# Attention and a gated feed-forward on one core: where batch 1's queries and two of its x are turned, and when the later batches are loaded

## The chip, the cores and the metric

The kernel runs on one core of a Trainium2 chip. The metric is the time of one execution on the device in microseconds (us), lower is better. TensorE multiplies matrices, VectorE, ScalarE and GpSimd work on tiles, SyncE issues transfers. The profile calls them PE (and PEld for its weight loads), DVE, ACT, POOL and SP.

## What is computed

q, k and v have the shape 4 x 8 x 768 x 64 (batch, head, position, width). Each position sees its neighbours less than 16 positions away, and 24 block summaries: the elementwise maximum of 32 keys, with the mean of 32 values. The result goes through two weight matrices with a gate between them.

```
k_sum = k.reshape(B, H, nb, block, D).max(axis=3)
v_sum = v.reshape(B, H, nb, block, D).mean(axis=3)
scores_l = scale * q @ k.T                 # kept where |i - j| < 16
scores_s = scale * q @ k_sum.T + log(32)
a = softmax(concat(scores_l, scores_s))
x = a @ concat(v, v_sum)                   # to (B * S, H * D) = (3072, 512)
h = x @ w_in                               # 512 -> 2048
out = (h / (1 + exp(-beta * h))) @ w_out   # 2048 -> 512
```

## The kernel before

The order on every engine is written by hand. Heads are taken in pairs, so each batch has four pairs g = 0..3, and a pair's two heads of width 64 fill the 128 partitions. Batch 0 has a path of its own at the start (lines 622 to 690). The loop over b at line 723 then runs the feed-forward of batch b as a main list of TensorE pieces, and between these pieces, at times given as numbers, it puts the attention of batch b + 1 (at_time, line 726). A piece with a smaller number is written earlier; the numbers only order the program, and each engine takes its instructions in that order and waits for their operands. Two kinds of main pieces alternate: the rising ones (h_group, h_ps at line 545, followed by the gate on ScalarE at line 557) and the falling ones (o_part, o_ps at line 576, followed by a copy and an output store at lines 595 and 596). For batch 0 the lists start at dn0 (the falling matmuls of the first half), up1 and dn1 (rising and falling of the second half); for the later batches the rising stage starts at 0 and the falling one at up.

The attention of a pair takes these steps:

- Loads. k, q and v come through POOL's queue, which also converts them to bf16. load_run (line 91) brings long runs: a partition holds six consecutive positions, both heads in one transfer. load_row (line 97) brings one position of one head per row, in two transfers per pair. load_v (line 103) brings v shifted by 16 rows, ve. load_1 (line 692) issues batch 1's loads, load_next (line 714) those of batches 2 and 3.
- Keys and queries are turned so that the width stands on the partitions: kw and qt. In batch 1 this is done on TensorE (turn, line 265: 12 transposes into pk or pq, line 276), and a copy (line 277) carries them out. In batches 2 and 3, cross (line 286) does it with two DMA transposes on SP's queue, one for k, one for q.
- max_k and rows_k (lines 293 and 303) make the block maxima and place them beside the keys, on VectorE.
- copy_v (line 312) makes vo, a second copy of v shifted by 16 rows across partitions. In batch 1 by eight DMAs on SP's queue, in batches 2 and 3 by VectorE.
- mean_v (line 319) takes the block means on TensorE (vm_ps, line 324); rows_v (line 348) places them with eight copies on VectorE (line 353).
- scores (line 449) multiplies queries with keys (s_ps, line 459) and takes the exponential on ScalarE (line 460), mask (line 480) multiplies with the band on VectorE (line 482), av (line 494) multiplies with v (av_ps, line 502), norm (line 506) divides into x_nat (line 512).
- x_transpose (line 515) turns x for the feed-forward, xT. Batch 1: six transposes on TensorE per pair (px, line 526) and a copy on ScalarE. Batches 2 and 3: one DMA transpose on SP's queue (line 521).

All of batch 1's k and q share the buffers k_all and q_all with batch 2's, so batch 2's loads of a pair wait until batch 1's have been turned. POOL's loads take eight completion semaphores in turn, so each of them waits for the landing of the eighth before it.

Of the kernel before, what the change touches and what calls it, by code (L numbers as in the profile page):

```python
# [12 lines left out]
def kernel(  # L13
# [10 lines left out]
    nc = tc.nc  # L24
# [18 lines left out]
    npair = H // 2  # L43
# [42 lines left out]
    nat = {}  # L86
    dve, act, pool = nc.vector.tensor_copy, nc.scalar.copy, nc.gpsimd.tensor_copy
# [3 lines left out]
    def load_run(nm, b, g, n=1, p0=0, p1=P, key=None):  # L91
        t = qk_bufs[nm][p0:p1, 2 * g:2 * (g + n)]
        nc.gpsimd.dma_start(out=t, in_=(k_run if nm == "k" else q_run)[b, p0:p1, 2 * g:2 * (g + n)])  # L93
        for i in range(n):
            nat[(key or nm, b, g + i)] = t[:, 2 * i:2 * i + 2]

    def load_row(nm, b, g):
        t = qk_bufs[nm][:, 2 * g:2 * g + 2].rearrange("p h f -> p (h f)").rearrange("p (c h d) -> p c h d", h=2, d=D)
        for h in range(2):
            nc.gpsimd.dma_start(out=t[:, :, h], in_=(k_row if nm == "k" else q_row)[b, g, :, h])  # L100
        nat[(nm, b, g)] = t

    def load_v(b, g):
        lo, hi = PC * g + 1, min(PC * (g + 1) + 1, HC)
        src = v_rows[b, lo * P - W:hi * P - W].rearrange("(c p) d -> p c d", p=P)
        nc.gpsimd.dma_start(out=ve_bufs[b % 2][:, lo:hi, 0:D], in_=src)  # L106
# [142 lines left out]
    def flat_k(b, g):  # L249
        return kw_of(b, g)[:, 0].rearrange("p c f -> p (c f)")  # L250
# [33 lines left out]
        turn(nm, b, g, flat_q(g)[:, lo:hi], copy, tag)  # L284

    def cross(b, g):
        kt, qn = nat.pop(("k", b, g)), nat.pop(("q", b, g))
        nc.sync.dma_start_transpose(out=flat_k(b, g)[:, W:W + S].rearrange("p (c f) -> p c f", f=P),
                                    in_=kt.rearrange("p c h d -> p (c h d)"))
        nc.sync.dma_start_transpose(out=qt_bufs[g].rearrange("p m r f -> p m (r f)"),  # L290
                                    in_=qn.rearrange("p c h d -> p (c h d)"))

# [222 lines left out]
    def x_transpose(key, m0, n, tag, copy):  # L515
        b, g = key[:2]
        if b not in xT:
            xT[b] = xt_pool.tile([P, k1, S], bf16, name="xT", tag="xT")
        x = x_nat.pop(key)
        if b > 1:  # L520
            nc.sync.dma_start_transpose(out=xT[b][:, g, :].rearrange("p (c f) -> p c f", f=P),
                                        in_=x.rearrange("p c h d -> p (c h d)"))
            return
        px = psum([P, n * P], bf16, "px", tag)
        for c in range(n):
            nc.tensor.transpose(px[:, c * P:(c + 1) * P], x[:, c].rearrange("p h d -> p (h d)"), identity)  # L526
        copy(out=xT[b][:, g, m0 * P:(m0 + n) * P], in_=px[:])
# [94 lines left out]
    for nm, n, copy, src in (("k", P, dve, k_f32), ("q", HP, act, q_f32)):  # L622
        t = nat[(nm, 0, 0)] = qk_bufs[nm][0:n, 0:2]
# [67 lines left out]

    def load_1(g):
        load_run("k", 1, g)
        load_run("q", 1, g)
        if g == npair - 1:
            load_v_first(1)
            load_v_last(1)
            for i in range(npair):
                load_v(1, i)

    GT, OT = 1.3, 0.865

    def run(main, side):
        side.sort(key=lambda z: z[0])
# [16 lines left out]
    for b in range(B):  # L723
        side = []

        def at_time(t, f, *a):
            side.append((t, lambda: f(*a)))

        us = [u for u in range(len(units)) if units[u][0] == b]
        main, t = [], 0.0  # L730
        if b == 0:
            starts = []
            for u in us:
                starts.append(t)
                for i in range(2 if u == 0 else 0, NG[u]):
                    main.append((t, lambda u=u, i=i: h_group(u, i)))
                    t += GT
                starts.append(t)
                todo = [(ms, q) for q in range(4) for ms in range(HM)] if u == 0 else [(ms, q) for ms in range(HM) for q in range(4)]
                for ms, q in todo:  # L740
                    main.append((t, (lambda ms=ms, q=q: o_quarter(0, ms, q)) if u == 0 else (lambda u=u, ms=ms, q=q: o_part(u, ms, q, 4))))
                    t += OT
            up0, dn0, up1, dn1 = starts
            us_rest = []
        else:
            us_rest = us
        for u in us_rest:
            for i in range(NG[u]):
                first = range(k1 - 1, k1) if i < 2 else range(k1)
                main.append((t, lambda u=u, i=i, first=first: h_group(u, i, first)))  # L750
                t += GT
        up = t
        for u in us_rest:
            for ms in range(units[u][2] * HM):
                for p in range(4):
                    main.append((t, lambda u=u, ms=ms, p=p: o_part(u, ms, p, 4)))
                    t += OT
        if b + 1 < B:
            main += [(t + i, lambda i=i: h_group(us[-1] + 1, i, range(k1 - 1))) for i in range(2)]
        nxt = b + 1  # L760
        pairs = tuple(range(npair))
        if b == 0:
            def part(n, f, *a):
                at_time(dn0 + OT * (n - 0.5), f, *a)

            for g in pairs:
                at_time(0.1 + 1.3 * g, rows_k, 0, g, HM)
                at_time(dn0 - GT - 0.1 if g < 2 else dn0 - 0.4, prep_q, 0, g, dve, "q2")
                at_time(dn0 - 0.3, load_1, g)
                if g > 1:  # L770
                    at_time(dn0 - 2 * GT, copy_v, 0, g, HM, dve)
                    at_time(dn0 - 2 * GT, rows_v0, g, dve)
            part(-0.1, load_table, ACTF.Exp)
            for g in pairs:
                part((0.2, 3)[g // 2], scores2, g)
                part((1.1, 3.2)[g // 2], mask2, g)
            for n in range(k2):
                part((-0.05, 1, 3.1, 4.5)[n // 4], scale_w_out, n)
            for gg in range(2):
                key = (1, 2 * gg, 2)  # L780
                part((4, 6)[gg], av2, key)
                part((4, 6)[gg], norm_x, key, 1 + gg)
            part(7.5, turn_x, (1, 0, 2), act)
            part(9.5, turn_x, (1, 2, 2), act)
            part(9.6, load_table, ACTF.Silu)
            for g in pairs:
                t = up1 + 0.3 + 2.2 * g
                at_time(t, prep_k, 1, g)
                at_time(t, prep_q, 1, g)
                at_time(t + 0.5, max_k, 1, g)  # L790
                at_time(t + 0.5, rows_k, 1, g)
                at_time(up1 + 3.0, copy_v, 1, g, 0, nc.sync.dma_start)
                at_time(up1 + 8.7, rows_v, 1, g)
            at_time(up1 + 8.6, mean_v, 1, pairs)
            at_time(dn1 - 0.1, load_table, ACTF.Exp)

            s_at = [dn1 + OT * (n - 0.5) for n in (0, 3, 5, 6)]
            a_at = [dn1 + OT * (n - 0.5) for n in (5, 6, 8, 9)]
            x_at = [t + 2.5 * OT for t in a_at]
        elif nxt < B:  # L800
            for g in pairs:
                t = (0.65, 1.95, 5.85, 9.75)[g]
                at_time(t, copy_v, nxt, g)
                at_time(t, cross, nxt, g)
                at_time(3.9 + 3.9 * g, max_k, nxt, g)
                at_time(3.9 + 3.9 * g, rows_k, nxt, g)
            at_time(15.3, mean_v, nxt, pairs)
            for g in pairs:
                at_time(15.4, rows_v, nxt, g)
            s_at = [up + 4.0 * g for g in pairs]  # L810
            a_at = [up + 4.0 * (g + 1) for g in pairs]
        if nxt < B:
            for g in pairs:
                for par in range(2):
                    at_time(s_at[g], scores, nxt, g, par)
                    at_time(s_at[g], mask, nxt, g, par)
                at_time(a_at[g], av, (nxt, g), nch)
                at_time(a_at[g], norm, (nxt, g), nch)
                if nxt > 1:
                    at_time(a_at[g], x_transpose, (nxt, g), 0, nch, "big", dve)  # L820
                else:
                    at_time(x_at[g], x_transpose, (nxt, g), 0, nch, "t", act)
        if nxt + 1 < B:
            for g in pairs:
                at_time((up1 + 5.0 if b == 0 else 1.0) + (2.5 if b == 0 else 4.5) * g, load_next, nxt + 1, g)
        run(main, side)


# [28 lines left out]
```

## Time and profile before

| | |
|---|---|
| median of 3 runs | 216.81 us (216.42 to 216.91) |
| the profiled execution | 215.99 us, its span 214.3 us |
| busy, PE / ACT / DVE / POOL | 206.3 / 122.1 / 104.1 / 77.7 us |
| moved by DMA | 25.88 MB, mean 121 GB/s |
| rising matmuls (L545) | 85.6 us |
| falling matmuls (L576 and L607) | 73.1 + 11.5 us |

The span runs from the first to the last instruction. Rows of the chain give the start in us, the length and what ran or was waited for; rows of a timeline the same with engine, line, operation and operands. Transfers are shown by their issue, with the time to landing beside them.

### The profile page before, as it was taken

The page shows a single profiled execution, that of the slowest core. Times are in us where ns is not written, and L with a number is a line of the kernel's source. Part 1 is how long each engine was busy: PE and PEld are TensorE (multiplying, and loading weights), DVE is VectorE, ACT ScalarE, POOL GpSimd, SP SyncE. Part 2 cuts the span into 40 slices and gives each one's busy share as a digit, 9 for nine tenths or more (in the row PEclk, how much of TensorE's full clock was granted, in tenths as well). Part 3 has the DMA queues.
Part 4 walks back from the last instruction along what each step waited for, and adds up shares of the span by engine and source line. Part 5 has one row for each costly group of instructions (what it writes and reads, how often), then busy time and mean ns, then how long its engine had stood idle before and what let it go on. Part 6 is the DMA issues. An engine that isn't in the chain of part 4 may idle for free.

```text
span 214.3 us, 5128 instructions
## 1 busy us (share of the span) xinstructions
PE 206.3 (96%) x2115; PEld 115.9 (54%) x2134; DVE 104.1 (49%) x299; ACT 122.1 (57%) x170; POOL 77.7 (36%) x113
## 2 busy tenths in 40 slices
PE   7999989999999999999999999999999999999994
PEld 2567654556655556655545466555554466654442
DVE  5768939808899729475544426182454000002120
ACT  2775977197788587668443187757342477650000
POOL 7996989496799308976000000000000000000000
PEclk9999999999999999999999999999999999999999
DMA  6999999999999999999934358400433300001212
GB/s 155 175 144 195 198 206 207 201 176 239 186 157 170 141 123 147 148 137 138 167 98 137 86 127 135 85 3 0 135 89 86 110 29 0 3 0 49 99 49 98
DMA packets 84087, 25.88 MB, mean 121 GB/s; under 512 B 70224, under 2 KB 81120, under 8 KB 84064
## 3 DMA queue, kind: packets, MB, share of 16 engines
q0 software_dynamic: 60272, 13.34, 76.2%
q1 hardware_dynamic: 23504, 11.82, 24.7%
q10 hardware_dynamic: 288, 0.39, 0.6%
q8 instruction: 16, 0.26, 0.5%
q14 instruction: 7, 0.06, 0.1%
HBM read 27.27 MB, written 6.29 MB: 157 GB/s over the span
## 4 chain that ended last, share of the span: by engine, by line
PE 82%; DMA 9%; POOL 4%; issue 1%; DVE 1%
PE h_ps L545 34%; PE o_ps L576 34%; DMA w_out_sb<-in_moe_w_out_dram 6%; PE o_ps L607 5%; DMA w_in_sb<-in_moe_w_in_dram 3%; PE av_ps L502 3%; PE s_ps L459 3%; POOL ve L106 2%; PE pk L276 1%; PE px L526 1%; PE vm_ps L324 1%; PE pq L276 1%; POOL q_all L93 1%; PE av_ps L491 0%; POOL near L144 0%
## 5 line engine op out<-in xcount | busy, mean ns | idle before, releaser
L545 PE MATMUL h_ps<-xT,w_in_sb 128*128 128x384 bf16 x512 | 85.6, 326 | 0.0
L576 PE MATMUL o_ps<-w_out_sb,h_sb 128*128 128x512 bf16 (+2 forms) x336 | 73.1, 369 | 2.0 <-issue 1.7
L557 ACT ACTIVATE h_sb<-h_ps,beta_sb 128x768 bf16<-128x768 f32 (+1 forms) x80 | 59.2, 772 | 22.6 <-PE h_ps L545 22.4
L545 PEld LDWEIGHTS <-w_in_sb 128*128 128x128 bf16 x512 | 49.3, 98 | 33.0
L576 PEld LDWEIGHTS <-h_sb 128*128 128x128 bf16 x352 | 32.4, 98 | 35.2
L460 ACT ACTIVATE attn<-s_ps 128x768 bf16<-128x768 f32 x24 | 18.1, 808 | 10.4 <-PE s_ps L459 10.4
L595 DVE COPY o_sb<-o_ps 128x512 f32<-128x512 f32 x5 | 3.5, 691 | 38.5 <-PE o_ps L576 38.5
L595 ACT COPY o_sb<-o_ps 128x512 f32<-128x512 f32 x15 | 8.8, 587 | 18.5 <-PE o_ps L576 12.7
L106 POOL DMA_DIRECT2D ve<-in_v_dram x16 | 17.1, 1074 | 1.8 <-DMA k_all<-in_k_dram 0.9
L482 DVE TENSOR_TENSOR attn<-attn,band 128x768 bf16<-128x768 bf16 x24 | 13.1, 554 | 7.5 <-ACT attn L460 6.0
L100 POOL DMA_DIRECT2D k_all<-in_k_dram x16 | 13.7, 860 | 7.7 <-DMA kw<-k_all 5.8
L100 POOL DMA_DIRECT2D q_all<-in_q_dram x16 | 13.6, 857 | 4.4 <-DMA ve<-in_v_dram 3.3
L296 DVE TENSOR_TENSOR half<-kw 128x384 bf16<-128x384 bf16 x16 | 5.9, 367 | 15.2 <-DMA kw<-k_all 15.0
L607 PE MATMUL o_ps<-w_out_sb,h_sb 128*128 128x512 bf16 x45 | 11.5, 379 | 1.1 <-DVE w_out_sb L235 0.7
L511 DVE RECIPROCAL r<-av_ps 128x12 f32<-128x12 f32 x12 | 2.8, 232 | 19.6 <-PE av_ps L502 19.6
L277 DVE COPY qt<-pq 128x384 bf16<-128x384 bf16 (+1 forms) x11 | 7.5, 696 | 9.5 <-PE pq L276 8.7
L512 DVE TENSOR_TENSOR x_nat<-av_ps,r 128x768 bf16<-128x768 f32 x12 | 11.5, 957 | 0.4
L588 ACT COPY o_sb<-o_ps 128x384 f32<-128x384 f32 x1 | 0.5, 478 | 19.0 <-PE o_ps L576 19.0
L317 DVE COPY vo<-ve 64x780 bf16<-64x780 bf16 (+3 forms) x20 | 8.9, 445 | 0.4
L502 PEld LDWEIGHTS <-attn 128*64 128x64 bf16 x288 | 5.5, 111 | 5.1 <-issue 3.0
L306 DVE COPY kw<-kw 128x192 bf16<-128x192 bf16 (+2 forms) x32 | 7.5, 277 | 0.0
L607 PEld LDWEIGHTS <-h_sb 128*128 128x128 bf16 x48 | 4.3, 97 | 5.8 <-issue 0.9
(115 smaller groups left out, 200.3 us busy)
## 6 DMA issues: line engine op xcount, KB each, us to landing
out_dram<-o_sb SPq DMA_DIRECT2D x23, 256.0 KB, 2.2
ve<-in_v_dram POOLq DMA_DIRECT2D x12, 192.0 KB, 6.9
w_in_sb<-in_moe_w_in_dram POOLq DMA_DIRECT2D x8, 256.0 KB, 8.3
w_out_sb<-in_moe_w_out_dram POOLq DMA_DIRECT2D x4, 512.0 KB, 12.4
q_all<-in_q_dram POOLq DMA_DIRECT2D x17, 96.0 KB, 6.3
k_all<-in_k_dram POOLq DMA_DIRECT2D x16, 96.0 KB, 6.9
k_all<-in_k_dram POOLq DMA_DIRECT2D x5, 192.0 KB, 8.1
q_all<-in_q_dram POOLq DMA_DIRECT2D x5, 192.0 KB, 7.2
```

Of the source, the lines that this page charges most:

```text
L100: nc.gpsimd.dma_start(out=t[:, :, h], in_=(k_row if nm == "k" else q_row)[b, g, :, h])
L106: nc.gpsimd.dma_start(out=ve_bufs[b % 2][:, lo:hi, 0:D], in_=src)
L317: copy(out=dst, in_=src)
L460: nc.scalar.activation(out=a.rearrange("p m h f -> p h m f"), in_=sv, func=ACTF.Exp, scale=scale)
L482: nc.vector.tensor_mul(out=a, in0=a, in1=band[:, par])
L502: nc.tensor.matmul(ov[par * QT:(par + 1) * QT, h, m], a[:, par, m, h], t[:, PC * g + nch * h + m0 + m], start=True, stop=True)
L512: nc.vector.tensor_mul(out=x.rearrange("p m h d -> p h m d"), in0=ov[:, :, :, 0:D], in1=r[:, :, :, None].to_broadcast([P, 2, n, D]))
L545: nc.tensor.matmul(big[:, j, 0:MG], w_in_sb[:, ki, ni * P:(ni + 1) * P], xT[b][:, ki, tok:tok + MG], start=(ki == 0), stop=(ki == k1 - 1))
L557: nc.scalar.activation(out=hb.rearrange("p (k m) -> p k m", m=MG), in_=big[:, j:j + w, 0:MG], func=ACTF.Silu, scale=beta_sb[:, ni:ni + 1])
L576: nc.tensor.matmul(o_ps[:, c0:c1], h_bufs[(u, ni * w // k2)][:, ni % (k2 // w), ms * P:(ms + 1) * P], w_out_sb[:, ni, c0:c1], start=(ni == ...
L595: (act if u + 1 < len(units) else dve)(out=o_sb[:], in_=o_ps[:])
L607: nc.tensor.matmul(o_ps, h_bufs[(u, ni * w // k2)][:, ni % (k2 // w), ms * P:(ms + 1) * P], w_out_sb[:, ni], start=(ni == 0), stop=(ni == ...
```

## The change

In batch 1 the queries are loaded by row, after k and after the first two loads of v, and turned by DMA (cross_q, cut out of cross). The shift of v moves from SP's queue to POOL and VectorE. The x of pairs 0 and 1 is turned by DMA. The loads of batches 2 and 3 are put at later numbers. In batches 2 and 3 the block means and their row copies move from 15.3 to 20.7, directly ahead of the first scores at 20.8, and the fourth pair's maximum from 15.6 to 22.0.

```
     def cross(b, g):
-        kt, qn = nat.pop(("k", b, g)), nat.pop(("q", b, g))
+        kt = nat.pop(("k", b, g))
         nc.sync.dma_start_transpose(out=flat_k(b, g)...)
+        cross_q(b, g)
+
+    def cross_q(b, g):
+        qn = nat.pop(("q", b, g))
         nc.sync.dma_start_transpose(out=qt_bufs[g]...)
...
-        if b > 1:
+        if b > 1 or g < 2:
             nc.sync.dma_start_transpose(out=xT[b][:, g, :]...)
...
     def load_1(g):
         load_run("k", 1, g)
-        load_run("q", 1, g)
         if g == npair - 1:
             load_v_first(1)
             load_v_last(1)
             for i in range(npair):
                 load_v(1, i)
+                if i == 1:
+                    load_row("q", 1, 0)
+            for i in range(1, npair):
+                load_row("q", 1, i)
...
+    RK = (3.9, 7.8, 11.7, 22.0)
...
-                at_time(t, prep_q, 1, g)
+                at_time(up1 + (6.0, 9.1, 9.2, 9.3)[g], cross_q, 1, g)
...
-                at_time(up1 + 3.0, copy_v, 1, g, 0, nc.sync.dma_start)
+                at_time(up1 + 6 + 0.1 * g, copy_v, 1, g, 0, pool if g % 2 else dve)
...
-                at_time(3.9 + 3.9 * g, max_k, nxt, g)
-                at_time(3.9 + 3.9 * g, rows_k, nxt, g)
-            at_time(15.3, mean_v, nxt, pairs)
+                at_time(RK[g], max_k, nxt, g)
+                at_time(RK[g], rows_k, nxt, g)
+            at_time(20.7, mean_v, nxt, pairs)
             for g in pairs:
-                at_time(15.4, rows_v, nxt, g)
+                at_time(20.75, rows_v, nxt, g)
...
-                if nxt > 1:
+                if nxt > 1 or g < 2:
                     at_time(a_at[g], x_transpose, (nxt, g), 0, nch, "big", dve)
...
-                at_time((up1 + 5.0 if b == 0 else 1.0) + (2.5 if b == 0 else 4.5) * g, load_next, nxt + 1, g)
+                at_time((up1 + 10.3 if b == 0 else 9) + (0.5 if b == 0 else 4.5) * g, load_next, nxt + 1, g)
```

SP's queue in batch 1, before, from the last two of the eight shifts of v to the first transpose of batch 2. The first three output stores (line 613) stand ahead of the shifts. vo1 and ve1 are the shifted copy and v of batch 1, kw0 is the turned keys of pair 0.

```order
L317 DMA vo1_81<-ve1_79 64x780
L317 DMA vo1_81<-ve1_79 32x780
L596 DMA out_0_dram<-o_sb_1323 128x512
L596 DMA out_0_dram<-o_sb_1379 128x512
L596 DMA out_0_dram<-o_sb_1565 128x512
L288 DMA_TRANSPOSE kw0_82<-k_all_90 128x6x128
```

The same place in the changed kernel; qt0 to qt3 are the turned queries of the four pairs.

```order
L617 DMA out_0_dram<-o_sb_994 128x512
L294 DMA_TRANSPOSE qt0_86<-q_all_91 128x6x128
L294 DMA_TRANSPOSE qt1_87<-q_all_91 128x6x128
L294 DMA_TRANSPOSE qt2_88<-q_all_91 128x6x128
L294 DMA_TRANSPOSE qt3_89<-q_all_91 128x6x128
L600 DMA out_0_dram<-o_sb_1265 128x512
L525 DMA_TRANSPOSE xT_1365<-x_nat6_1361 128x6x128
L525 DMA_TRANSPOSE xT_1365<-x_nat6_1427 128x6x128
L600 DMA out_0_dram<-o_sb_1331 128x512
L600 DMA out_0_dram<-o_sb_1503 128x512
L288 DMA_TRANSPOSE kw0_82<-k_all_90 128x6x128
```

The eight shifts of v are gone from this queue. Four transposes of q stand in their place, each waiting for its row-wise loads, and two of x stand between the output stores.

VectorE in batch 1 around the fourth pair's maximum (half, km) in the changed kernel; vo_81 and ve_79 are the shifted copy and v, vm_110 the block means.

```order
L312 COPY kw_84<-km 128x6x24 x2
L321 COPY vo_81<-ve_79 64x780
L321 COPY vo_81<-ve_79 32x780
L321 COPY vo_81<-ve_79 64x780
L321 COPY vo_81<-ve_79 32x780
L300 TENSOR_TENSOR half<-kw_85 128x384
L305 TENSOR_REDUCE km<-half 128x24
L310 COPY kw_85<-kw_85 128x6x64
L310 COPY kw_85<-kw_85 128x6x32
L312 COPY kw_85<-km 128x6x24 x2
L331 CAST vm_110<-vm_ps 128x2x64
L357 COPY ve_79<-vm_110 32x780
```

The four shifts of v (pairs 0 and 2) are new there; before, a copy of turned queries (line 277) stood ahead of each pair's maximum.

VectorE in batch 2, before, from the last row copy of the means to the first masks (attn).

```order
L353 COPY vo_80<-vm_109 32x780
L296 TENSOR_TENSOR half<-kw_85 128x384
L301 TENSOR_REDUCE km<-half 128x24
L306 COPY kw_85<-kw_85 128x6x64
L306 COPY kw_85<-kw_85 128x6x32
L308 COPY kw_85<-km 128x6x24 x2
L482 TENSOR_TENSOR attn<-attn,band 128x768 x2
```

The same place in the changed kernel.

```order
L357 COPY vo_80<-vm_109 32x780
L486 TENSOR_TENSOR attn<-attn,band 128x768 x2
L300 TENSOR_TENSOR half<-kw_85 128x384
L305 TENSOR_REDUCE km<-half 128x24
L310 COPY kw_85<-kw_85 128x6x64
L310 COPY kw_85<-kw_85 128x6x32
L312 COPY kw_85<-km 128x6x24 x2
```

The masks now follow the row copies directly, and the fourth pair's maximum stands behind them. On TensorE the 28 matmuls of the means move from three quarters of the rising stage to its end, directly ahead of the first scores. On POOL, batch 2's loads now come after four copies of v.

## Prediction

> **What bounds the kernel now.** I read the page first (busy time by engine, and the shares of the chain that ended last), then who waited for whom on TensorE, then the chain in order of time, and only then the other engines around the places that the change touches.
>
> ```profile
> PE 206.3 (96%) x2115; PEld 115.9 (54%) x2134; DVE 104.1 (49%) x299; ACT 122.1 (57%) x170; POOL 77.7 (36%) x113
> PE 82%; DMA 9%; POOL 4%; issue 1%; DVE 1%
> PE o_ps L607 <- DVE w_out_sb L235: 0.7, 1, 0.7
> ```
>
> TensorE is busy for 206.3 of 214.3 us. After the start-up its longest single wait is 0.7 us, at 32 us, and nothing that the change edits runs before that. So from 32 us on a microsecond of TensorE work taken away is a microsecond gained, as long as no operand comes late. The chain in order of time (start, length, what) shows the stretch in question:
>
> ```profile
> 47.39 0.34 PE pq L276 x12
> ...
> 56.58 0.34 PE pq L276 x12
> ...
> 60.25 0.46 PE s_ps L459 x24
> ...
> 63.40 0.46 PE s_ps L459 x24
> ...
> 65.69 0.50 PE av_ps L502 x24
> 66.20 0.46 PE s_ps L459 x24
> ...
> 68.12 0.46 PE s_ps L459 x24
> ...
> 69.55 0.34 PE px L526 x6
> ...
> 71.25 0.44 PE px L526 x6
> ...
> 72.55 0.50 PE av_ps L502 x24
> 73.05 0.16 issue
> ...
> 76.60 15.60 PE h_ps L545 x96
> ```
>
> The chain runs through TensorE without a break. Batch 1's first scores stand at 60.25, its first products with v at 65.69, and batch 2's rising matmuls start at 76.60.
>
> **What goes from TensorE.** Four query turns of 12 transposes (first and last shown) are worth 4 x 0.34 = 1.36 us. Two turns of x are worth 0.34 + 0.44 = 0.78 us. The second of these stands behind products with v. Where no turn stands there, an issue gap of 0.16 us follows (73.05), so I count 0.33 for it. Sum: 1.36 + 0.34 + 0.33 = **2.03 us**. The copies that carried these turns out of PSUM go too (VectorE for q, ScalarE for x). Neither was on the chain, so they count only where they make room.
>
> **The transposed queries.** They now need the row-wise loads, which POOL issues behind k and half of v, and then a DMA transpose on SP's queue. No transpose runs in this stretch before, so its cost is bounded by the rows of batch 2 (a busy stretch) and the x of batch 2:
>
> ```profile
> L290 SPq DMA_TRANSPOSE qt<-q_all x4: 1210/1242/1441, 79.3 to 88.4; - x4
> DMA to landing us min/median/max: 2.8/6.1/9.5
> ...
> L521 SPq DMA_TRANSPOSE xT<-x_nat x1: 1211/1211/1211, 104.7 to 104.7; - x1
> DMA to landing us min/median/max: 4.3/4.3/4.3
> ```
>
> One lands 2.8 us after its issue with little beside it, and 9.5 us at the end of a row of eight among loads. 4.3 is a single one next to loads that are ending. For the loads, the rows are the keys of batch 1 and two of the v loads:
>
> ```profile
> L93 POOL DMA_DIRECT2D k_all<-in_k_dram x4: 718/726/748, 33.1 to 37.3; - x4
> DMA to landing us min/median/max: 6.9/8.3/9.0
> ...
> L106 POOL DMA_DIRECT2D ve<-in_v_dram x1: 1062/1062/1062, 42.8 to 42.8; - x1
> DMA to landing us min/median/max: 6.3/6.3/6.3
> ...
> L106 POOL DMA_DIRECT2D ve<-in_v_dram x1: 1012/1012/1012, 55.4 to 55.4; - x1
> DMA to landing us min/median/max: 7.6/7.6/7.6
> ```
>
> The first key lands at 33.1 + 6.9 = 40.0, the last at 37.3 + 9.0 = 46.3. These are four k and three q in one row, 1.05 us each. Without the q between them the keys are in at 43.2. From the landing at 49.1 to that at 63.0 the queue moved five loads of v and four half pairs (one head each, half a v load), the size of seven v loads: 2.0 us each. Output stores and the eight v shifts by DMA ran beside that. The shifts go, the stores stay. The other bound is POOL's own 1.0 us of issue for one. I take 1.7, near the measured one. The new row is v, v, q0, v, v, q1, q2, q3, each the size of one v load: q0 in at 43.2 + 3 x 1.7 = 48.3, q1 at 53.4, q2 at 55.1, q3 at 56.8. With 4.3 for a transpose they land at 52.6, 57.7, 59.4 and 61.1. Scores want them at the starts above less 1.36: 58.9, 62.0, 64.8 and 66.8. So they are 4 us or more early and I charge **0**. At the bad ends (2.0 and 9.5) q1 is there at 43.2 + 12.0 + 9.5 = 64.7, 2.7 us late.
>
> A rule speaks against this step. The Trainium skill, "DMA: Bandwidth & Descriptors", section "Issuing engines are not separate DMA queues", says that DMAs of every issuing engine end up on the same 16 DMA engines and interleave there. The trace agrees: the same transpose takes 2.8 or 9.5 us. By that rule my charge of nothing holds only while few loads run beside the transposes; the sum by it, at the bad ends, is that of the first rival below.
>
> SP waits in order. Behind the four transposes stand batch 1's output stores, the two transposes of x and batch 2's transposes, all wanted after 64 us.
>
> **VectorE in batch 1.** The shift of v by 16 rows moves from SP to POOL (pairs 1, 3) and VectorE (pairs 0, 2). The timeline of VectorE, and a copy of POOL half as wide:
>
> ```profile
> 55.59 0.86 DVE L308 COPY kw<-km 128x144 bf16<-128x144 bf16 x2
> ...
> 57.94 0.36 DVE L296 TENSOR_TENSOR half<-kw 128x384 bf16<-128x384 bf16 x1
> ...
> 59.67 0.29 DVE L327 CAST vm<-vm_ps 128x128 bf16<-128x128 f32 x1
> ...
> 63.90 2.35 DVE L482 TENSOR_TENSOR attn<-attn,band 128x768 bf16<-128x768 bf16 x4
> ...
> 68.80 0.96 DVE L512 TENSOR_TENSOR x_nat<-av_ps,r 128x768 bf16<-128x768 f32 x1
> ...
> 82.52 0.95 DVE L317 COPY vo<-ve 64x780 bf16<-64x780 bf16 x2
> ...
> 128.55 0.73 DVE L317 COPY vo<-ve 64x780 bf16<-64x780 bf16 x2
> ...
> L317 POOL COPY vo<-ve 64x390 bf16<-64x390 bf16 x2 | 1.0, 506 | 0.1
> ```
>
> The third pair's keys are done at 56.45, or 55.8 when two query turns (0.68) no longer stand ahead on TensorE. Two shifts follow, 0.73 to 0.95 each: 57.3 to 57.7. Maximum and copies of pair 3 take 59.67 - 57.94 = 1.73, the means and their rows 63.90 - 59.67 = 4.23, the first two masks half of 2.35. They end at 64.4 to 64.8. TensorE wants them at 65.69 - 1.36 = 64.3. Before, they ended 0.6 us early; now they are late by 0.1 to 0.5, and I charge **0.3 us**. The removed query copies leave VectorE idle rather than shorten this chain, since the masks stand behind all of it.
>
> POOL's four shifts cost some 4 us by the row above at twice the width (an estimate). Batch 2's loads stand behind them and start at about 53.5 instead of 47. They are as large as twelve v loads: 20 to 24 us, so in at 74 to 78. Their transposes begin at about 76.60 - 2.0, one pair after the other, and have until batch 2's scores, 20 us on: no charge.
>
> **The two x by DMA.** The second is divided at about 69.5 (68.80 + 0.96, a little earlier). With 4.3 it lands at 73.8. The rising matmuls want it at 76.60 - 2.03 + 0.3 = 74.9: no charge, 1 us of room. At 9.5 it is 4 us late; 6.1 makes it 0.7 late.
>
> **Means ahead of the scores (batches 2 and 3).** TensorE does the same work, but the eight row copies now stand on VectorE between the means and the first masks:
>
> ```profile
> 92.20 0.52 PE vm_ps L324 x28
> ...
> 98.03 0.46 PE s_ps L459 x24
> ...
> 102.91 0.50 PE av_ps L502 x24
> ...
> 138.71 0.52 PE vm_ps L324 x26
> ...
> 96.59 0.37 DVE L353 COPY vo<-vm 32x780 bf16<-32x780 bf16 x1
> ...
> 101.12 1.26 DVE L482 TENSOR_TENSOR attn<-attn,band 128x768 bf16<-128x768 bf16 x2 [2.46 <-ACT attn L460]
> ...
> 142.26 0.37 DVE L353 COPY vo<-vm 32x780 bf16<-32x780 bf16 x1
> ```
>
> From the start of the means, the rows end after 96.96 - 92.20 = 4.76 us in batch 2 (POOL is issuing loads) and 142.63 - 138.71 = 3.92 in batch 3. Masks take 1.26 more: 6.02 and 5.18. TensorE wants them after 0.52 + (102.91 - 98.03) = 5.40. Batch 3 is in time by 0.2, batch 2 late by up to 0.62; how much depends on whether POOL still issues then. I charge the middle, **0.3 us**. Pair 3's maximum, moved behind these masks, has pair 0's products to hide behind and its own scores are 12 us off. In the Trainium skill, "SBUF — State Buffer", section "A bandwidth-pool intuition that's wrong (but worth ruling out)", the reason would be that such copies and POOL's descriptor writing exclude each other. The trace's longer copies under POOL's loads fit (4.76 against 3.92 us); by that rule the full 0.6 would fall due whenever the two coincide, and the sum would be 215.7.
>
> **Sum.** -2.03 + 0.3 + 0.3 = -1.4 us. The profiled execution took 215.99 us (span 214.3 and 1.7 around it), so 214.6 by its own measure. It was 0.8 below the median of the runs shown. From that, 216.81, I forecast **215.4 us**.
>
> **Rivals.**
> 1. *Late queries (slower).* At 2.0 us a load and 9.5 a transpose, TensorE stands 2.7 us before pair 1's scores: 215.4 + 2.7 = 218.1. It turns the sign once pair 1's transpose lands past 62.0 + 1.4 = 63.4. For it: TensorE has no other work queued there, and the DMA rule cited above. Against: the four come singly, not as the eighth of a row. Chance 0.24, of it 0.17 slower, 0.03 same.
> 2. *Late x.* At 6.1 to 7 us the second x holds TensorE 0.7 to 1.6 us before 74.9: 216.1 to 217.0. For it: batch 2's loads, now later, run just there. Chance 0.12, a third of it same.
> 3. *The turns go but VectorE sets the pace of batch 1's falling stage*, so what TensorE saves there returns as waits, 1.0 to 2.0 more than charged: 216.4 to 217.4. For it: VectorE's chain above is one run from 57.94 to the end of the masks at 66.25. Against: it catches up once the first masks are through. Chance 0.10, a third each way.
>
> **Numbers.** The forecast has 0.54, with 214.8 (no stall) to 216.0. Faster by over 0.2% (0.43 us, about what a measurement of this kernel can tell from no change) is 0.54 + 0.04 + 0.08 + 0.04 = 0.70, same 0.10, slower 0.20. The range goes from 214.5, the end without stalls less some scatter, up to 217.4, which leaves out the worst of the first rival.
>
> **What would show it.** No pq of batch 1 and two px fewer on TensorE, and the rising stage of batch 2 starting 1.7 us earlier; waits of TensorE before av_ps of 0.3 us in batches 1 and 2 for the mask. Wrong would be a wait of s_ps on a DMA of qt (rival 1), of h_ps on xT (rival 2), or several waits on masks in batch 1 (rival 3).

## The result and the profile after

The changed kernel takes 217.43 us in the median of 20 runs (216.31 to 220.4), the kernel before 216.59 (215.73 to 217.93) beside it. The ratio is 1.0044, with a 95% interval of 1.0024 to 1.0065: slower by 0.4%. The forecast was 215.4 us, and the upper end of the range, 217.4, just misses the median. Medians and ranges, here and below, are of all runs, while the ratios leave out the slow ones, those over 1.5% above the fastest of the same kernel (2 of the changed kernel's 20), so a ratio can differ from the quotient of the medians.

The page of the changed kernel, busy time by engine and the shares of the chain that ended last:

```profile
span 215.2 us, 5010 instructions
PE 203.5 (95%) x2055; PEld 113.8 (53%) x2074; DVE 105.2 (49%) x299; ACT 120.5 (56%) x168; POOL 85.7 (40%) x121
PE 78%; DVE 10%; DMA 7%; issue 2%; ACT 1%; POOL 1%
```

TensorE lost 60 matmuls, the turns of four q and two x, and 2.8 us of busy time, yet the span grew from 214.3 to 215.2 us. VectorE now has 10% of the chain. Who TensorE waited for, longest first among the waits that the change made:

```profile
PE h_ps L549 <- DMA xT<-x_nat: 2.0, 1, 2.0
...
PE av_ps L506 <- DVE attn L486: 0.2, 1, 0.2
```

One wait of 2.0 us, for a transpose of x, is as large as all that was taken away. The chain in order of time (start, length, what) shows where it stands:

```profile
45.75 1.30 PE h_ps L549 x8
...
68.04 0.96 DVE x_nat L516
...
69.03 8.25 DMA xT<-x_nat
...
77.31 20.80 PE h_ps L549 x127
...
102.69 1.04 DVE attn L486 x2
...
103.78 0.57 PE av_ps L506 x21
...
124.04 20.80 PE h_ps L549 x128
...
170.43 20.80 PE h_ps L549 x128
```

Pair 1's x is divided by 69.00 and its transpose issued at 69.03, slightly earlier than forecast. It lands 8.25 us later, and TensorE, which had begun batch 2's rising stage at 75.0 with one matmul, goes on at 77.31. In batch 2 the masks (L486) end directly before the products with v start: there TensorE's chain leads through VectorE too.

The same chain of the kernel before:

```profile
45.64 1.30 PE h_ps L545 x8
...
123.11 15.60 PE h_ps L545 x96
...
169.61 20.80 PE h_ps L545 x128
```

From the start of the second half's rising matmuls (45.64) to batch 2's rising stage (76.60) the kernel before took 30.96 us, and from there to batch 3's (123.11) 46.51. Changed, these are 31.56 and 46.73. Without the wait (1.98 us) and the one matmul ahead of it (0.16) the first would be 31.56 - 1.98 - 0.16 = 29.4. That is still 0.5 above 30.96 - 2.03. The timeline of TensorE shows where these 0.5 us go, at batch 1's first two products with v:

```profile
64.40 0.22 PE L506 MATMUL av_ps<-ve,attn 128*64 128x65 bf16 x1
64.87 0.22 PE L506 MATMUL av_ps<-vo,attn 128*64 128x65 bf16 x1 [0.25 <-DVE attn L486]
```

The second waits for a mask and starts 0.47 us after the first; in the kernel before they start 0.01 us apart. The list of waits counts only 0.2 of it, because the first product is still running for a part of that time.

The two transposes of x, and the first and last of those of q, on SP's queue:

```profile
L525 SPq DMA_TRANSPOSE xT<-x_nat x2: 1221/1232/1244, 66.9 to 69.0; - x2
DMA to landing us min/median/max: 7.7/8.0/8.2
...
L294 SPq DMA_TRANSPOSE qt<-q_all x1: 2307/2307/2307, 47.7 to 47.7; - x1
DMA to landing us min/median/max: 10.2/10.2/10.2
...
L294 SPq DMA_TRANSPOSE qt<-q_all x1: 1298/1298/1298, 58.3 to 58.3; - x1
DMA to landing us min/median/max: 7.0/7.0/7.0
```

### The profile page after: what moved, and what is told of

Same layout as the page of the kernel before. It is cut to its first block, busy times and chain, and to the rows that moved or that the text cites. A ratio compares the mean times of both kernels' runs of the same rounds, so it can differ in the third digit from the quotient of the medians.

```text
span 215.2 us, 5010 instructions
## 1 busy us (share of the span) xinstructions
PE 203.5 (95%) x2055; PEld 113.8 (53%) x2074; DVE 105.2 (49%) x299; ACT 120.5 (56%) x168; POOL 85.7 (40%) x121
## 4 chain that ended last, share of the span: by engine, by line
PE 78%; DVE 10%; DMA 7%; issue 2%; ACT 1%; POOL 1%
PE h_ps L549 36%; PE o_ps L580 27%; PE o_ps L611 5%; DMA xT<-x_nat 4%; DMA q_all<-in_q_dram 3%; DVE ve L357 2%; PE av_ps L506 2%; DVE attn L486 2%; PE s_ps L463 1%; DVE vo L357 1%; DVE x_nat L516 1%; DVE vo L321 1%; ACT h_sb L561 1%; PE px L447 1%; PE pk L276 1%
## 5 line engine op out<-in xcount | busy, mean ns | idle before, releaser
L580 PEld LDWEIGHTS <-h_sb 128*128 128x128 bf16 x352 | 32.4, 98 | 35.5
L100 POOL DMA_DIRECT2D q_all<-in_q_dram x24 | 20.3, 862 | 5.4 <-DMA qt<-q_all 1.9
L486 DVE TENSOR_TENSOR attn<-attn,band 128x768 bf16<-128x768 bf16 x24 | 12.5, 552 | 0.6
L321 DVE COPY vo<-ve 64x780 bf16<-64x780 bf16 (+3 forms) x24 | 10.9, 453 | 0.5
L310 DVE COPY kw<-kw 128x192 bf16<-128x192 bf16 (+2 forms) x32 | 8.4, 303 | 0.0
L331 DVE CAST vm<-vm_ps 128x128 bf16<-128x128 f32 x3 | 0.8, 273 | 13.8 <-PE vm_ps L328 13.8
L506 PE MATMUL av_ps<-ve,attn 128*64 128x65 bf16 x144 | 7.2, 197 | 0.0
```

Source lines behind the costliest of these rows:

```text
L321: copy(out=dst, in_=src)
L486: nc.vector.tensor_mul(out=a, in0=a, in1=band[:, par])
L506: nc.tensor.matmul(ov[par * QT:(par + 1) * QT, h, m], a[:, par, m, h], t[:, PC * g + nch * h + m0 + m], start=True, stop=True)
L580: nc.tensor.matmul(o_ps[:, c0:c1], h_bufs[(u, ni * w // k2)][:, ni % (k2 // w), ms * P:(ms + 1) * P], w_out_sb[:, ni, c0:c1], start=(ni == ...
```

## The experiments

Theory A: batch 2's loads run beside the two transposes of x, delay them, and TensorE waits 2.0 us at the start of batch 2's rising stage. Rival B: VectorE sets the pace, and the wait on xT only stands where its chain ends. Rival C: with its loads later, batch 2 would wait somewhere in any case. The stage lengths below are differences of chain rows like those above, each from one profiled execution.

**x back on TensorE.** The conditions on g are taken out again in x_transpose and in the plan.

```
-        if b > 1 or g < 2:
+        if b > 1:
```

> All four x of batch 1 turned on TensorE again, the rest as changed. Theory A (the second x lands late and holds TensorE 2.0 us): the wait goes, the two turns come back with 0.67 us, so 1.3 us below the changed kernel, about 216.1, 0.2% under before. Rival B (VectorE sets the pace of batch 1's falling stage, the wait on xT only stands where its chain ends): the time stays or grows by 0.67, 217.4 to 218.1. Rival C (any transfer that batch 2 needs early is late since its loads moved): the wait moves on to another DMA, 217 to 217.5.

Measured: 216.8 us against 216.93, ratio 0.9972 (0.9929 to 1.0015): by the total not to be told from the kernel before. The stage can tell.

```profile
PE av_ps L506 <- DVE attn L486: 0.5, 2, 0.3
...
46.52 1.31 PE h_ps L549 x8
...
76.93 20.80 PE h_ps L549 x128
```

No wait on a DMA stands after the start, which speaks against C. The stage takes 30.41 us, 1.15 less than changed, where A gave 1.3. Against the kernel before it saves 0.55, though the four turns of q are worth 1.36: TensorE waits for masks at batch 1's first two products with v, 0.5 us by the list of waits and 0.8 by the stage. So B holds for some tenths of a microsecond.

**Only the x by DMA, on the kernel before.** The same two conditions are put into the kernel before.

> The kernel before with nothing but the x of pairs 0 and 1 of batch 1 by DMA. If such a transpose is late at this place whatever runs beside it, TensorE waits about 2 us: 216.6 - 0.67 + 2.0 = 217.9. If it is late only because batch 2's loads were moved into this stage (here they land by 74.4 us), it lands within 4 to 6 us, in time or nearly: 215.9 to 216.5.

Measured: 215.97 us, ratio 0.9949 (0.9913 to 0.9985): faster.

```profile
L521 SPq DMA_TRANSPOSE xT<-x_nat x2: 1407/1642/1877, 67.7 to 70.0; - x2
DMA to landing us min/median/max: 6.0/6.6/7.2
...
45.84 1.30 PE h_ps L545 x8
...
76.13 15.60 PE h_ps L545 x96
```

The stage takes 30.29 us, 0.67 less than before: all of the two turns is gained, though the transposes take 7.2 and 6.0 us. The second lands at 70.0 + 6.0 = 76.0, just in time for the rising stage at 76.13. So x by DMA pays with the loads where they were, and it is late only together with the rest of the change. But even here a transpose took well over 4.3 us.

**Means, row copies and the fourth maximum at their old places.**

```
-    RK = (3.9, 7.8, 11.7, 22.0)
+    RK = (3.9, 7.8, 11.7, 15.6)
-            at_time(20.7, mean_v, nxt, pairs)
+            at_time(15.3, mean_v, nxt, pairs)
-                at_time(20.75, rows_v, nxt, g)
+                at_time(15.4, rows_v, nxt, g)
```

> The changed kernel with the means, their row copies and the fourth pair's maximum of batches 2 and 3 at their old places. Theory A: the 2.0 us wait on xT stays and only the 0.3 us before batch 2's first products with v go: about 0.3 us below the changed kernel, 217.1. Rival B (VectorE's order there is the main cost): 0.8 us or more below it, at or under before.

Measured: 216.75 us, ratio 0.9995 (0.9955 to 1.0035), not to be told from before. Some tenths of a microsecond are looked for in the stage.

```profile
PE h_ps L549 <- DMA xT<-x_nat: 1.5, 1, 1.5
```

```profile
76.93 15.60 PE h_ps L549 x95
...
123.43 15.60 PE h_ps L549 x96
```

The wait on xT stays. From batch 2's rising stage to batch 3's it takes 46.50 us, as before (46.51), against 46.73 in the changed kernel, so the means cost that one 0.2 us there.

**Without batch 2's loads of pairs 2 and 3.** load_next returns early for these two.

```
+        if b == 2 and g > 1:
...                                 # two lines that only name the buffers
+            return
         load_v(b, g)
```

> The changed kernel without the loads of pairs 2 and 3 of batch 2 (it goes on with what the buffers hold, so part of batch 2's input is left out). Theory A in the form that loads beside them delay the two x transposes: they land 3 to 5 us after their issue instead of 7.7 and 8.3, no wait of TensorE on xT, and the profiled span is 2 us shorter than that of the changed kernel. If instead the queue's order or the late division delays them, the wait of 2 us stays.

Measured: 214.96 us in one run, span 213.3 us, 1.9 below the changed kernel's.

```profile
L525 SPq DMA_TRANSPOSE xT<-x_nat x2: 1211/1211/1211, 67.0 to 69.1; - x2
DMA to landing us min/median/max: 2.7/3.5/4.2
```

The issue is where it was, the landing comes after 4.2 us (first) and 2.7 us (second) instead of 7.7 and 8.2, and no wait on xT is left. The loads beside the transposes make the difference, not the order of SP's queue nor a late division.

**The queries alone** (x on TensorE and means at their old places, both edits above).

> Of the change only the queries, the shift of v and the later loads are left: x on TensorE, means at their old places. The prediction's sum for this part: -1.36 for the turns, 0.3 for the masks of batch 1, so 1.0 under before (ratio 0.995). Theory A with the waits found so far (masks of batch 1 0.5 us): 0.9 under before. Rival C (the later loads hold batch 2's rising stage or its scores): no gain or slower.

Measured: 215.88 us against 216.66, ratio 0.9957 (0.9924 to 0.9991): faster.

```profile
45.59 1.30 PE h_ps L549 x8
...
75.40 15.60 PE h_ps L549 x96
...
121.90 15.60 PE h_ps L549 x96
```

The stage takes 29.81 us, 1.15 less than before, so 0.2 of the 1.36 is lost here, again at the first two products with v. The next stage takes 46.50, as before: rival C falls, the later loads alone cost batch 2 nothing. The same code up to there took 30.41 in the first experiment, so this loss varies from 0.2 to 0.8 between executions.

**Only pair 0's x by DMA** (g < 1 in place of g < 2).

> The changed kernel, but of batch 1's x only pair 0 by DMA, pair 1 on TensorE. Theory A: the first x was issued at 66.9 and landed at 74.6, just before the rising stage asks for it at 75.0, so the wait falls from 2.0 to 0 to 0.5 us, and one turn comes back with 0.33: 1.2 to 1.7 us under the changed kernel. If every transpose at this place holds TensorE by 2 us, it stays.

Measured: 215.8 us, ratio 0.9943 (0.991 to 0.9976): faster.

```profile
L525 SPq DMA_TRANSPOSE xT<-x_nat x1: 1220/1220/1220, 67.3 to 67.3; - x1
DMA to landing us min/median/max: 7.6/7.6/7.6
```

It takes as long as in the changed kernel, but was issued 1.7 us earlier than pair 1's. It lands at 74.9, in time, and no wait on xT is left. So the second x alone is what comes late.

**The loads held back.** GpSimd writes into the second x after its transpose has read it, and the loads of pairs 2 and 3 stand behind that write.

```
+            if (b, g) == (1, 1):
+                nc.gpsimd.memset(x[:, 0, 0], 0.0)
...
-    (up1 + 10.3 ...) + (0.5 if b == 0 else 4.5) * g
+    (up1 + 10.3 ...) + ((0, 0.5, 5.2, 5.3)[g] if b == 0 else 4.5 * g)
```

> The changed kernel, complete, with batch 2's loads of pairs 2 and 3 held back until the second x of batch 1 has been read by its transpose (a small write of GpSimd into that x stands ahead of them). Theory A (loads beside the transposes): both land 3 to 5 us after their issue, no wait on xT, 2.0 us under the changed kernel and about 1.2 under before. Rival: the loads held back are then late for batch 2 itself, by a wait on kw or qt before its scores, and the gain is lost there.

Measured: 215.15 us, ratio 0.9926 (0.9896 to 0.9956): faster, and it does all of the work.

```profile
L525 SPq DMA_TRANSPOSE xT<-x_nat x2: 1212/1328/1443, 66.6 to 68.8; - x2
DMA to landing us min/median/max: 3.3/4.1/4.8
...
45.97 1.30 PE h_ps L551 x8
...
74.93 20.80 PE h_ps L551 x128
...
122.03 20.80 PE h_ps L551 x128
```

POOL issues no load from 64.7 us until the small write at 72.18. The transposes land after 4.8 us (first) and 3.3 us (second). The stage takes 28.96 us, 2.0 less than before: everything that the change takes from TensorE is gained once the loads stand aside. The next stage takes 47.10, 0.6 more than before. TensorE waits there for masks, not for kw or qt, so the rival did not happen; that the means ahead of the scores are the reason is tested in the last run below.

**The loads held back, means at their old places.**

> As the run with the loads held back, and the means of batches 2 and 3 at their old places. If the 0.3 us before batch 2's products with v is due to the means alone, 0.3 us under that run, 1.5 under before (ratio 0.993). If the later v of batch 2 makes the means late at their old place, TensorE waits there instead, and it is slower than that run.

Measured: 216.22 us, ratio 0.995 (0.9915 to 0.9984), an interval that holds the 0.993 too. The stage from batch 2's rising matmuls to batch 3's decides. Below are its two ends, who TensorE waited for, and VectorE's timeline ahead of batch 2's first masks:

```profile
74.90 10.19 PE h_ps L551 x63
...
122.96 15.60 PE h_ps L551 x96
...
PE av_ps L506 <- DVE attn L486: 1.3, 2, 1.0
...
93.85 0.36 DVE L300 TENSOR_TENSOR half<-kw 128x384 bf16<-128x384 bf16 x1 [1.97 <-DMA kw<-k_all]
...
100.04 0.36 DVE L300 TENSOR_TENSOR half<-kw 128x384 bf16<-128x384 bf16 x1
...
101.63 1.01 DVE L486 TENSOR_TENSOR attn<-attn,band 128x768 bf16<-128x768 bf16 x2
```

It takes 48.06 us, 1.0 more than in the run with the loads held back, where 0.3 less was expected. The third pair's maximum waits for its keys until 93.85, the row copies follow, then the fourth pair's maximum and copies (100.04 to the masks at 101.63), and only then the masks. So the masks are late, but not for the reason that the expectation gave: TensorE made the means at 90.4 without a wait. VectorE had stood waiting for the third pair's keys, and the fourth maximum, 1.6 us, then stood ahead of the masks.

**The loads held back, means early, the fourth maximum late** (of the three lines above only the one of RK is put back to the change's).

> As the run with the loads held back, with the means and their row copies of batches 2 and 3 at their old, earlier place, but the fourth pair's maximum left behind the first masks. If the 1.0 us wait of the run before it comes from that maximum alone (it stood ahead of the masks on VectorE and waited for the late keys of pair 3), that wait is gone here. Then nothing of the means stands ahead of the first masks, TensorE does not wait before batch 2's products with v, and the time is 0.2 to 0.3 us under the run with the loads held back: 214.9, ratio 0.991. If the row copies are what was late, a wait on the mask stays.

Measured: 216.34 us beside 217.62 for the kernel before, ratio 0.9906 (0.9863 to 0.9949): faster than before. Its interval overlaps that of the run with the loads held back, so the totals do not show the expected 0.2 to 0.3 us. The profiled execution had a granted clock of 0.992, against 1.000 in the changed kernel's, and came late to the second half (48.33), so only batch 2's stage is read from it, in which 96 rising matmuls take 15.60 us as in the other runs.

```profile
78.25 15.60 PE h_ps L551 x96
...
99.68 0.46 PE s_ps L463 x24
...
104.56 0.50 PE av_ps L506 x24
...
124.76 15.60 PE h_ps L551 x96
```

From scores to products it takes 4.88 us and the stage 46.51, both as before: nothing waits for masks there. VectorE's order is the same as in the run with the loads held back; only TensorE's means come earlier. So the 0.6 us of that run came from the means directly ahead of the scores, as far as this one execution shows.

## Why the prediction was wrong

- **What goes from TensorE, 2.03 us: right.** The run with the loads held back shows 2.00 in the stage, the x alone 0.67.
- **The transposed queries in time: right, with less room than stated.** The first took 10.2 us and landed at 57.9 instead of 52.6, the last at 65.3 instead of 61.1. Scores stood at 58.95 and 67.3, so these two had 1 to 2 us left and not 4 or more. TensorE has no wait on qt, so rival 1 did not happen. The charge of 0 held only because there was room: 4.3 us was too little for each of the four (6.0 to 10.2), the same slip that costs 2.0 us at the x.
- **VectorE in batch 1, 0.3 us: right in kind.** It was 0.5 in the changed kernel, and 0 to 0.8 in the others. Rival 3, waits of 1 to 2 us more than charged, did not happen.
- **The two x by DMA: this step failed.** "With 4.3 it lands at 73.8", said the prediction, "no charge, 1 us of room". It took 8.25 us and landed at 77.3; the term is 2.0 us and not 0. The mechanism was the second rival, given a chance of 0.12 and 0.7 to 1.6 us. The row of 4.3 came from a place where loads were ending. Here loads ran beside the transposes to their end, and the prediction could have known it: by its own estimate batch 2's loads were in at 74 to 78, after the 73.8 at which it had the second x land. That estimate was also too early:

```profile
L106 POOL DMA_DIRECT2D ve<-in_v_dram x1: 1072/1072/1072, 54.7 to 54.7; - x1
DMA to landing us min/median/max: 5.8/5.8/5.8
...
L100 POOL DMA_DIRECT2D q_all<-in_q_dram x2: 873/878/884, 72.5 to 73.3; - x2
DMA to landing us min/median/max: 8.6/9.3/10.0
```

  These are batch 2's first v and its last queries. The first lands at 60.5, the last at 73.3 + 10.0 = 83.3: eleven loads' size in 22.8 us, 2.1 each. The rate was the one measured in the prediction (2.0). But it counted from the first issue and left out the 5.8 us until the first landing, and so had all in at 74 to 78. The rule cited there from the Trainium skill, "DMA: Bandwidth & Descriptors", section "Issuing engines are not separate DMA queues", that the DMAs of all issuing engines interleave on the same 16 DMA engines, was weighed for the queries alone. The second x fits it: 2.7 us without the loads and 8.2 with them. That the loads are the cause is shown by leaving them out and by holding them back; at which part of the way they meet the transposes no run here shows.
- **Means ahead of the scores, 0.3 us: right.** The stage of batch 2 grew by 0.2 us in the changed kernel and by 0.6 in the run with the loads held back, and batch 3's did not (124.04 to 170.43 against 123.11 to 169.61). In three runs with the means early the stage is as before (46.50, 46.50 and 46.51). That the fourth maximum belongs behind the masks once loads are late was not seen.

The sum was -1.4 us; with 2.0 for the x it is +0.6. The stages of the profiled executions show +0.60 (31.56 against 30.96) and +0.22 (46.73 against 46.51), and the medians +0.84.

## What to carry to other kernels

Moving work from the bounding engine to DMA is worth its time only if the transfer still lands in time with the loads that run beside it. Take its duration from a row inside such loads, and count when those loads end from their first landing. A load that is wanted late can be made to wait for a short transfer that is wanted soon: here that turned 0.4% slower into 0.7% faster. Where an engine works in order, what is wanted later belongs behind what the bounding engine waits for.

## What was not expected

Programs that are the same up to there reach the second half's rising stage at times that differ by a microsecond from one profiled execution to the next: 45.51 us with the means back, 46.52 with x on TensorE, 45.97 with the loads held back. In nine of the eleven profiled executions the chain ahead of that start leads through a load of w_out, but in the changed kernel's it does not, so what sets it stays open. The scatter is as large as what the change is worth; stage lengths told the kernels apart where totals did not.
